# Tile 0's last product by column halves, with the second batch's attention spread through it

## The chip, the core and the metric

The kernel runs on one core of one Trainium2 chip. The core has a tensor engine (TensorE, PE in the profile: matmuls; its weight loads are shown as PEld), a vector engine (DVE), a scalar engine (ACT), a general engine (GpSimd, shown as POOL) and an engine that only issues transfers here (SyncE, SP). Sixteen DMA engines carry the transfers. Data lies in SBUF (128 partitions); matmuls write to PSUM, eight banks of 128 partitions by 512 fp32 values.

The metric is the device time of one execution, in microseconds. Before the change it is 351.59, the median of 3 runs (351.44 to 352.12).

## The reference

Attention over 8 batches and 8 heads, 576 tokens of width 64, causal by blocks of 64, then a gated feed-forward layer over all 4608 tokens.

```python
scores = scale * np.matmul(q, k.transpose(0, 1, 3, 2))   # q, k, v: (8, 8, 576, 64)
mask = block_i >= block_j                                # blocks of 64 positions
scores = np.where(mask, scores, -1000000000.0)
attn = np.exp(scores - np.max(scores, axis=-1, keepdims=True))
attn = attn / (np.sum(attn, axis=-1, keepdims=True) + 1e-09)
attn_out = np.matmul(attn, v)
x = attn_out.transpose(0, 2, 1, 3).reshape(4608, 512)
gate = np.maximum(x @ w_gate, 0.0)                       # w_gate, w_val: (512, 1536)
val = x @ w_val
return (gate * val @ w_out).astype(np.float32)           # w_out: (1536, 512)
```

All inputs and the output are float32; the kernel multiplies in bf16.

## The kernel before

**Tiles and steps.** The 512 first tokens of batch j make up tile j (0 to 7); the last 64 tokens of all batches make up a ninth tile. The feed-forward work is a generator, `ffn_gen` (L942), that hands out TensorE's matmuls one step at a time. Tile 0 has 144 steps: 96 products with the gate and value weights (L948: for each of 12 blocks of d_ff four gate products and four value products, the gate through ACT's relu at L958, their product on DVE at L968 as `hT`), and then 48 out products (`out_mm`, L1180) of 128 tokens by 512 columns: `hT` against `wo`, the bf16 copy of w_out. A finished group of 12 is copied by DVE to a buffer `ob` (`finish`, L1189) and stored later (`put`, L657; for tile 0 through the list `late`, from ACT's queue). In tile 0 the 48 run as groups two at a time, a third of the inner dimension in turn (L1201).

**The attention of later batches is spread between the steps.** The order is written out by hand for all five engines. A dictionary `AT` (L1338) gives each act a place, counted in steps; a loop at the end (L1780) emits the acts by place, and `ffn` (L1227) emits the steps that lie between. Places below 0 are before the first step. `HOW` (L1581) names the engine and the PSUM banks of each act. The names that matter here:

- `Lq`, `Lv`, `E1q`, `E1v`, `E2q`, ...: loads of q, k and v of batches 0, 1, 2 from SP's queue; `w{i}{g}` (i = 0 to 2, g = 0, 1): loads of w_out (`load_w_out`, L389); `T0` to `T2`: loads of the batches' tails. All loads go into a pool of ten staging buffers.
- `cq`, `cv`, `cg`, `cw`, `ev`, `q4`, `q6`, `tc`: casts of such loads to bf16, mostly on POOL (L198, L223, L231, L397).
- `m{hp}` (`mains_1`, L1329): TensorE transposes of q and k of a pair of heads of batch 1 (L284), with the copies out of PSUM (L293).
- `p{r}{i}` (`part`, L424): for batch 0, scores and exponential in three parts. `s{r}` and `e{r}`: for later batches the scores of a pair of heads (`visit`, L442; TensorE at L465) and their exponential on ACT (L470, L477). r is 4 x batch + pair of heads, so batch 1 has r = 4 to 7. Two parts of the scores go to the two double banks "sc"; the third goes, one half each, to two banks that `thirds` (L436) names.
- `c{r}`: memsets of the masked corners (`corners`, L523; L1241). `a{r}`, `b{r}`: the products with v of the first and second head (`head_av`, L626; L600) and the division by the row sum on DVE (`normalise`, L533; L537, L539). `x{r}`: the transposes into `xT`, the input of the feed-forward layer (`to_xT_pe`, L636, or by DMA).
- `l3`, `lv3`: batch 3's loads, issued by POOL (L353). `W`, `D`: sums of w_out's quarters on POOL (L706, L709) and differences on DVE (L720), for tiles 7 and 8, which use a product scheme with fewer multiplications.

**PSUM.** Two double banks ("sc"), one bank "one", three banks "ffn" that rotate. Gate and value products use ffn banks and, for some value products, "one" or "sc".

**Queues.** SP issues its loads in the written order; a load also waits for the eighth load before it. POOL works through its casts in order, so a late load holds all casts behind it.

The function that loads and casts w_out:

```python
    def load_w_out(i, g):
        return load_w(
            wo[i][:, 2 * g : 2 * g + 2],
            moe_w_out[512 * i + 256 * g : 512 * i + 256 * g + 256],
        )
```

Of the kernel before, what the change touches and what calls it, by code (L numbers as in the profile page):

```python
# [17 lines left out]
def kernel(  # L18
# [10 lines left out]
    nc = tc.nc  # L29
# [359 lines left out]
    def load_w_out(i, g):  # L389
        return load_w(  # L390
            wo[i][:, 2 * g : 2 * g + 2],
            moe_w_out[512 * i + 256 * g : 512 * i + 256 * g + 256],
        )
# [42 lines left out]
    def thirds():  # L436
        return (
            psum_one.tile([128, 512], FP, name="one"),
            psum_ffn.tile([128, 512], FP, name="ffnp"),
        )  # L440

    def visit(r):  # L442

        b, hp = divmod(r, 4)
        at = attnT[r % 4]
        first = psum_sc.tile([128, 2, 512], FP, name="sc")
        second = psum_sc.tile([128, 2, 512], FP, name="sc")
        third = thirds()
        tails = b >= FIRST
        pieces = [(2, False), *((c, True) for c in range(4) if tails)]  # L450
        for c, tail in pieces + [(c, False) for c in (0, 1, 3)]:
            for hh in range(2):
                where = {
                    0: first[:, hh, :],
                    1: second[:, hh, 0:384],
                    3: second[:, hh, 384:512],
                    2: third[hh][:, 0:256],
                }
                if tail:
                    o = third[hh][:, 256 + 64 * c : 320 + 64 * c]  # L460
# [4 lines left out]
                nc.tensor.matmul(  # L465
                    o, kTm[b % 2][head_of(hh), c, hp, :], qT, start=True, stop=True
                )
# [12 lines left out]

        return exp_third, exp(first, 0), exp(second, 512)
# [460 lines left out]
    def ffn_gen():  # L942
        for j in range(B + 1):
# [245 lines left out]
            def finish(op, s, n0, n1):  # L1189
                ob = sb.tile([128, 512], FP, name="ob", bufs=5)[:, 0 : n1 - n0]  # L1190
                nc.vector.tensor_copy(ob, op)
                if store:
                    store.pop()()
                (store if j else late).append(lambda j=j: put(j, s, ob, n0, n1))
# [6 lines left out]
            groups = outs(j)  # L1201
            while groups:
                some = 2 if j == 0 and len(groups) == 4 else 1
                ops = [
                    psum_ffn.tile([128, 512], FP, name="ffnp")[:, 0 : n1 - n0]
                    for _, n0, n1 in groups[:some]
                ]
                for f0 in (0, 4, 8) if some == 2 else (0,):
                    for op, (s, n0, n1) in zip(ops, groups):
                        for f in range(f0, f0 + 4 if some == 2 else 12):  # L1210
                            out_mm(op, s, f, n0, n1)
                            if f == 11:
                                finish(op, s, n0, n1)
                            yield
                groups = groups[some:]
# [30 lines left out]
    with tc.manual_schedule(engines={E.PE, E.DVE, E.Activation, E.Pool, E.SP}):  # L1246
# [82 lines left out]
        def mains_1(hp):  # L1329
            engs, banks = HOW[f"m{hp}"]  # L1330
            if banks == "one":
                both = bank("one", BF)
                two = [both[:, 512 * t : 512 * t + 512] for t in range(2)]
            else:
# [6 lines left out]
            "cq4": -40,  # L1341
            "cq6": -39.5,
            "M1q": -39,
            "M1k": -38.5,
            "p01": -38,
            "c0": -37.5,
            "j3": -37,
            "p11": -36.5,
            "M2q": -36,
            "p10": -35.5,  # L1350
            "M2k": -35,
            "p12": -34.5,
            "j2": -34,
            "M3q": -33.5,
            "M3k": -33,
            "cv0": -32.5,
            "cv2": -32,
            "c1": -31.5,
            "p20": -31,
            "a0": -30.5,  # L1360
# [9 lines left out]
            "cg00/01": -25.5,  # L1370
            "p30": -25,
            "cv4a": -24.5,
            "cv4b": -24,
            "cg00/23": -23.5,
            "x1": -23,
            "p32": -22.5,
            "c2": -22,
            "c3a": -21.5,
            "c3b": -21,
            "cv6a": -20.5,  # L1380
            "a2": 3,
            "b2": 3.01,
            "cv6b": 3.02,
            "C1": 3.03,
            "a3": 6,
            "b3": 6.01,
            "x2": 6.02,
# [22 lines left out]
            "ev0a": 32.33,  # L1410
            "ev0b": 32.34,
# [18 lines left out]
            "w01": 32.1,  # L1430
            "w00": 32.11,
            "w11": 32.11,
            "w20": 32.12,
            "w10": 32.12,
            "E1v0": 32.16,
            "w21": 32.16,
            "E1q6": 32.19,
            "E1q4": 32.19,
            "E1v4": 32.19,
# [4 lines left out]
            "cw00": 32.3,  # L1444
            "cw10": 32.3,
            "cw01": 32.3,
            "cw21/0": 32.33,
            "cw11": 32.33,
            "cw20": 32.33,
            "q6": 32.36,  # L1450
            "q4": 32.36,
            "E2q4": 33.82,
            "ev4": 34.05,
# [9 lines left out]
            "cw21/1": 110.84,  # L1463
            "e4": 114.3,
            "c4": 116.83,
            "s5": 119.48,
            "a4": 120.37,
            "b4": 120.57,
            "e5": 121.28,
            "m2": 122.6,  # L1470
            "c5": 124.67,
            "E2v4": 125.35,
            "T2": 126.26,
            "a5": 127.05,
            "s6": 128.09,
            "e6": 128.35,
            "b5": 129.8,
            "c6": 131.42,
            "m3": 132.5,
            "x4": 135.4,  # L1480
            "x5": 135.8,
            "s7": 139.49,
            "a6": 139.55,
            "b6": 140.59,
            "e7": 141.27,
            "c7": 141.68,
            "x6": 145.48,
            "a7": 147.62,
            "b7": 147.81,
            "x7": 153,  # L1490
# [112 lines left out]
            "cw21/1": "dve",  # L1603
# [17 lines left out]
            "cw21/0": "pool",  # L1621
# [25 lines left out]
                for n in (  # L1647
                    "g00/01 g00/23 v00/01 v00/23 g01/01 g01/23 v01 g10 v10 g11 v11 "
                    "g20 v20 g21 v21/0 v21/1 w00 w01 w10 w11 w20 w21/0 w21/1"
# [165 lines left out]
```

## Time and profile before

| what | value |
|---|---|
| median of 3 runs | 351.59 us (351.44 to 352.12) |
| the profiled execution, its own time | 352.3 us |
| its span on the core | 350.5 us |
| mean granted TensorE clock | 0.999 |
| PE busy | 339.8 us (97%), 3210 instructions |
| DVE, ACT, POOL busy | 225.5 (64%), 185.2 (53%), 153.8 us (44%) |
| DMA | 50.02 MB, mean 143 GB/s |
| tile 0's first gate or value product, and the end of its last out product | 15.77 and 57.26 us |

The profile comes from one execution. Times in it are counted from the first instruction, in microseconds. "Busy" for an engine is the time in which at least one of its instructions ran; matmuls overlap in the pipeline, so the printed mean of one is longer than the distance from one to the next. In a line of a timeline the first two numbers are start and duration, followed by engine, line of the kernel, operation, output and inputs, shape and count; what stands in square brackets is the idle time before and what ended it.

Gate products (L948) are the largest group by time of all engines, 93.0 us in 338 recorded instructions; out products of the tiles that use L1181 take 23.2 us in 91.

### The profile page before, as it was taken

The page shows a single profiled execution, that of the slowest core. Times are in us where ns is not written, and L with a number is a line of the kernel's source. Part 1 is how long each engine was busy: PE and PEld are TensorE (multiplying, and loading weights), DVE is VectorE, ACT ScalarE, POOL GpSimd, SP SyncE. Part 2 cuts the span into 40 slices and gives each one's busy share as a digit, 9 for nine tenths or more (in the row PEclk, how much of TensorE's full clock was granted, in tenths as well). Part 3 has the DMA queues.
Part 4 walks back from the last instruction along what each step waited for, and adds up shares of the span by engine and source line. Part 5 has one row for each costly group of instructions (what it writes and reads, how often), then busy time and mean ns, then how long its engine had stood idle before and what let it go on. Part 6 is the DMA issues. An engine that isn't in the chain of part 4 may idle for free.

```text
span 350.5 us, 8275 instructions
## 1 busy us (share of the span) xinstructions
PE 339.8 (97%) x3210; PEld 208.2 (59%) x3254; DVE 225.5 (64%) x564; ACT 185.2 (53%) x297; POOL 153.8 (44%) x194
## 2 busy tenths in 40 slices
PE   8999999999999999999999999999999999999994
PEld 3544455545445568545855576556755687687673
DVE  4853455667529784467547772668567867986892
ACT  5933766687235862666355545555366525423521
POOL 2767556576598902590149203950300022213213
PEclk9999999999999999999999999999999999999999
DMA  8999989999999994999459974999510031003005
GB/s 240 295 353 373 352 224 248 222 148 155 184 185 153 144 182 98 138 147 169 62 134 141 104 135 123 127 131 150 121 47 17 16 94 50 2 2 121 1 2 120
DMA packets 155399, 50.02 MB, mean 143 GB/s; under 512 B 134464, under 2 KB 151744, under 8 KB 155360
## 3 DMA queue, kind: packets, MB, share of 16 engines
q0 software_dynamic: 70528, 8.98, 49.1%
q1 hardware_dynamic: 77520, 32.52, 44.0%
q10 hardware_dynamic: 7312, 8.00, 7.8%
q8 instruction: 25, 0.41, 0.5%
q14 instruction: 14, 0.11, 0.1%
HBM read 37.75 MB, written 9.44 MB: 135 GB/s over the span
## 4 chain that ended last, share of the span: by engine, by line
PE 77%; DMA 14%; POOL 3%; issue 2%; DVE 2%; ACT 1%; SPq 1%; POOLq 0%; ACTq 0%
PE ffnp L948 39%; PE ffnp L830 12%; PE one L830 5%; PE sc L1014 3%; DMA stage<-in_moe_w_out_dram 3%; PE sc L465 3%; DMA xT<-xnat 2%; DMA stage<-in_moe_w_val_dram 2%; PE one L465 2%; DMA stage<-in_v_dram 2%; DMA stage<-in_moe_w_gate_dram 2%; PE ffnp L600 2%; PE one L600 2%; PE ffnp L1181 2%; PE one L1014 2%
## 5 line engine op out<-in xcount | busy, mean ns | idle before, releaser
L958 ACT ACTIVATE gate_sb<-ffnp 128x512 bf16<-128x512 f32 x95 | 57.1, 605 | 74.8 <-PE ffnp L948 66.5
L948 PE MATMUL ffnp<-xT,wg 128*128 128x512 bf16 x338 | 93.0, 379 | 1.7 <-issue 0.6
L948 PE MATMUL ffnp<-xT,wv 128*128 128x512 bf16 x309 | 87.7, 380 | 1.0 <-DVE hT L968 0.3
L968 DVE TENSOR_TENSOR hT<-gate_sb,ffnp 128x512 bf16<-128x512 bf16 x76 | 51.9, 683 | 46.0 <-PE ffnp L948 27.0
L948 PEld LDWEIGHTS <-wv 128*128 128x128 bf16 x384 | 35.4, 98 | 38.2 <-issue 4.6
L470 ACT ACTIVATE attnT<-sc 128x1024 bf16<-128x1024 f32 x56 | 57.0, 1042 | 0.0
L948 PEld LDWEIGHTS <-wg 128*128 128x128 bf16 x384 | 35.7, 98 | 35.0 <-issue 1.7
L882 POOL TENSOR_TENSOR ob<-ob 128x512 f32<-128x512 f32 x7 | 9.6, 1370 | 101.7 <-ACT ob L879 53.3
L830 PEld LDWEIGHTS <-stage 128*128 128x128 bf16 x420 | 40.3, 98 | 6.0
L789 DVE TENSOR_TENSOR stage<-hT 128x512 bf16<-128x512 bf16 (+2 forms) x82 | 37.8, 493 | 0.9
L600 PEld LDWEIGHTS <-attnT 128*128 128x128 bf16 x640 | 26.7, 98 | 11.9 <-DVE attnT L1241 0.9
L830 PE MATMUL ffnp<-stage 128*128 128x256 bf16 x252 | 31.4, 273 | 0.0
L353 POOL DMA_DIRECT2D v_bf<-in_v_dram x30 | 24.1, 869 | 6.1 <-DVE recip L537 2.6
L477 ACT ACTIVATE attnT<-one 128x512 bf16<-128x512 f32 (+1 forms) x28 | 15.0, 536 | 21.1 <-PE ffnp L465 21.1
L353 POOL DMA_DIRECT2D q_bf<-in_q_dram x20 | 17.9, 907 | 16.7 <-DVE hT L968 9.7
L1181 PE MATMUL ffnp<-wo,hT 128*128 128x512 bf16 x91 | 23.2, 379 | 0.3
L465 PEld LDWEIGHTS <-kTm 64*128 64x128 bf16 x384 | 11.0, 94 | 15.1 <-issue 7.9
L1045 POOL TENSOR_TENSOR ob<-ob 128x512 f32<-128x512 f32 x6 | 7.6, 1266 | 23.2 <-ACT ob L1044 23.2
L353 POOL DMA_DIRECT2D k_bf<-in_k_dram x20 | 17.8, 927 | 0.0
L830 PEld LDWEIGHTS <-hT 128*128 128x128 bf16 x168 | 16.4, 98 | 1.9
L465 PE MATMUL sc<-qTm,kTm 64*128 64x512 bf16 (+1 forms) x168 | 16.8, 305 | 0.0
L879 ACT COPY ob<-ffnp 128x512 f32<-128x512 f32 x7 | 4.1, 585 | 22.1 <-PE ffnp L830 22.1
(194 smaller groups left out, 556.0 us busy)
## 6 DMA issues: line engine op xcount, KB each, us to landing
out_dram<-ob ACTq DMA_DIRECT2D x28, 256.0 KB, 2.3
stage<-in_moe_w_val_dram SPq DMA_DIRECT2D x6, 512.0 KB, 8.7
stage<-in_moe_w_gate_dram SPq DMA_DIRECT2D x6, 512.0 KB, 8.2
stage<-in_moe_w_out_dram SPq DMA_DIRECT2D x6, 512.0 KB, 10.5
q_bf<-in_q_dram POOLq DMA_DIRECT2D x20, 128.0 KB, 4.2
k_bf<-in_k_dram POOLq DMA_DIRECT2D x20, 128.0 KB, 5.2
v_bf<-in_v_dram POOLq DMA_DIRECT2D x20, 128.0 KB, 7.0
stage<-in_v_dram SPq DMA_DIRECT2D x19, 128.0 KB, 5.5
```

Of the source, the lines that this page charges most:

```text
L353: ins = nc.gpsimd.dma_start(dst, part_of)
L465: nc.tensor.matmul(o, kTm[b % 2][head_of(hh), c, hp, :], qT, start=True, stop=True)
L470: return lambda: nc.scalar.activation(at[:, :, lo : lo + 512], sc, AF.Exp, scale=scale)
L477: nc.scalar.activation(at[:, hh, 1024 : 1024 + w], third[hh][:, 0:w], AF.Exp, scale=scale)
L600: nc.tensor.matmul(av[:, p, :], at[:, col : col + 128], v_bf[b % 2][:, c, h, :], start=(p == 0), stop=(c == p), skip_group_check=True,)
L789: nc.vector.tensor_tensor(out=out.rearrange("p (c n) -> p c n", c=m), in0=a, in1=b, op=op)
L830: nc.tensor.matmul(to, sums.of(c)[which][:, 128 * p : 128 * p + 128], right, start=first, stop=(c == 5), skip_group_check=True,)
L948: nc.tensor.matmul(to, (wg, wv)[t][f // 4][:, c, 128 * (f % 4) : 128 * (f % 4) + 128], x[:, c], start=(c == 0), stop=(c == 3),)
L958: nc.scalar.activation(gate_sb, gate, AF.Relu)
L968: nc.vector.tensor_tensor(out=h, in0=gate_sb, in1=val, op=AX.mult)
L1014: nc.tensor.matmul(to[:, 256 * k : 256 * k + 256], left[:, c, 128 * k : 128 * k + 128], right[:, c], start=new and (k, c) == (0, 0), stop= ...
L1181: nc.tensor.matmul(op, hT[f][:, 128 * s : 128 * (s + 1)], wo[f // 4][:, f % 4, n0:n1], start=(f == 0), stop=(f == 11),)
```

## The change

Four things, in the order of the diff.

1. `load_w_out` loads 512 rows by 256 columns (4 x 256 elements to a partition, runs of 1 KB) instead of 256 rows by 512 columns (runs of 2 KB). A load is 512 KB either way. SP's order becomes: the three left halves, v's first half of batch 1, q and k of batch 1's last two pairs of heads, the right half of the first part, v's second half, the right halves of the second and third part. Before, all six loads of w_out stood ahead of these loads of batch 1. The casts on POOL follow in the new order; the last of them is no longer split with DVE.
2. Tile 0's out products are four groups of 24 matmuls of 256 columns: a group is a column half and two blocks of 128 tokens, all into one bank: "one" for the first three groups, an ffn bank for the last. A step is two of them. One copy on DVE ends a group, and `put_block` stores it (512 rows of 1 KB runs become 256 rows by 256 columns).
3. Batch 1's acts from `e4` to `x7` are at other places. Both halves of the third part of the scores are in ffn banks for batch 1. `m2` and `m3` use one ffn bank, with both copies on DVE (before on ACT). `x4` is copied by DVE (before ACT); the banks of `r4`, `r6` and `r7` differ.
4. Batch 0: `cv0` before `cq4` and `cq6`, `a0` before `p20` and `M3k`, `p32` before `p30`, `b2` a step later, `x2` before `b3`; the corner memsets `c1`, `c2`, `c3b` on POOL instead of DVE, `c3a` later.

From tile 1 on, all places are the same.

```diff
     def load_w_out(i, g):
-        return load_w(
-            wo[i][:, 2 * g : 2 * g + 2],
-            moe_w_out[512 * i + 256 * g : 512 * i + 256 * g + 256],
-        )
+        n = slice(256 * g, 256 * g + 256)
+        return load_w(wo[i][:, :, n], moe_w_out[512 * i : 512 * i + 512, n])
...
-    def thirds():
-        return (
-            psum_one.tile([128, 512], FP, name="one"),
-            psum_ffn.tile([128, 512], FP, name="ffnp"),
-        )
+    def thirds(r):
+        return [bank("ffn" if i or r // 4 == 1 else "one") for i in range(2)]
...
-            groups = outs(j)
+            for half, s0 in [(h, s) for h in range(2) for s in (0, 2)] if j == 0 else []:
+                op = bank("ffn" if (half, s0) == (1, 2) else "one")
+                order = [
+                    (f, s)
+                    for i in range(3)
+                    for s in (s0, s0 + 1)
+                    for f in range(4 * i, 4 * i + 4)
+                ]
+                for n, (f, s) in enumerate(order):
+                    nc.tensor.matmul(
+                        op[:, 256 * (s - s0) : 256 * (s - s0) + 256],
+                        hT[f][:, 128 * s : 128 * (s + 1)],
+                        wo[f // 4][:, f % 4, 256 * half : 256 * half + 256],
+                        start=(n == 0),
+                        stop=(f == 11),
+                        skip_group_check=True,
+                    )
+                    if n == 23:
+                        ob = sb.tile([128, 512], FP, name="ob", bufs=5)
+                        nc.vector.tensor_copy(ob, op)
+                        late.append(
+                            lambda s0=s0, half=half, ob=ob: put_block(
+                                0, s0 // 2, 256 * half, ob, 0, 2
+                            )
+                        )
+                    if n % 2:
+                        yield
+            groups = outs(j) if j else []
             while groups:
-                some = 2 if j == 0 and len(groups) == 4 else 1
...
-            "cq4": -40,
-            "cq6": -39.5,
...
+            "cv0": -40,
+            "cq4": -39.5,
+            "cq6": -39,
...
+            "M3q": -33,
+            "a0": -32.5,
+            "p20": -32,
+            "M3k": -31.5,
...
+            "w01": 32.132,
+            "E1v4": 32.135,
+            "cw21": 32.362,
+            "cw01": 32.352,
+            "ev4": 32.355,
+            "c5": 114,
+            "m3": 115,
+            "s6": 115.01,
+            "e6": 115.02,
+            "a5": 120,
+            "b5": 120.01,
+            "x4": 120.02,
+            "s7": 125,
+            "e7": 125.01,
+            "c6": 125.02,
+            "a6": 128,
+            "b6": 128.01,
+            "x5": 132,
+            "c7": 134,
+            "a7": 136,
+            "b7": 136.01,
+            "x6": 139,
+            "x7": 143,
+            "c4": 107,
+            "w00": 32.1,
+            "w10": 32.101,
+            "w20": 32.102,
+            "E1v0": 32.11,
+            "E1q4": 32.12,
+            "E1q6": 32.13,
+            "w11": 32.141,
+            "w21": 32.142,
...
+            "e4": 95.1,
+            "s5": 108.01,
+            "e5": 108.02,
+            "a4": 108.03,
+            "m2": 108.04,
+            "b4": 108.05,
...
-            "s5": 119.48,
-            "a4": 120.37,
-            "b4": 120.57,
...
-            "m2": (("act", "act"), ("sc", "ffn")),
-            "m3": (("act", "act"), "one"),
+            "m2": (("dve", "dve"), "ffn"),
+            "m3": (("dve", "dve"), "ffn"),
-            "r4": ("dve", "one", "ffn", ("act", "sc")),
+            "r4": ("dve", "ffn", "ffn", ("dve", "ffn")),
             "r5": ("dve", "ffn", "ffn", ("act", "ffn")),
-            "r6": ("dve", "ffn", "ffn", ("act", "sc")),
-            "r7": ("dve", "sc", "one", ("dve", "one")),
+            "r6": ("dve", "ffn", "ffn", ("act", "one")),
+            "r7": ("dve", "one", "sc", ("dve", "one")),
...
-            "c1": "dve",
-            "c2": "dve",
+            "c1": "pool",
+            "c2": "pool",
             "c3a": "dve",
-            "c3b": "dve",
+            "c3b": "pool",
```

More of the change, by code (lines that the diff above doesn't have):

```diff
@@ L447, in visit @@
         second = psum_sc.tile([128, 2, 512], FP, name="sc")
-        third = thirds()
+        third = thirds(r)
         tails = b >= FIRST
@@ L1193, in finish @@
                     store.pop()()
-                (store if j else late).append(lambda j=j: put(j, s, ob, n0, n1))
+                store.append(lambda j=j: put(j, s, ob, n0, n1))
             if j >= SEVEN:
@@ L1199, in ffn_gen @@
                 continue
-            groups = outs(j)
-            while groups:
-                some = 2 if j == 0 and len(groups) == 4 else 1
[L1204 to L1215, printed above, removed]
+            for half, s0 in [(h, s) for h in range(2) for s in (0, 2)] if j == 0 else []:
[25 more added lines that the diff above has]
+                        yield
@@ L1217, in outs @@
+            groups = outs(j) if j else []
+            while groups:
+                s, n0, n1 = groups.pop(0)
+                op = psum_ffn.tile([128, 512], FP, name="ffnp")[:, 0 : n1 - n0]
+                for f in range(12):
+                    out_mm(op, s, f, n0, n1)
+                    if f == 11:
+                        finish(op, s, n0, n1)
+                    yield
     def outs(j):
@@ L1330, in mains_1 @@
             engs, banks = HOW[f"m{hp}"]
-            if banks == "one":
-                both = bank("one", BF)
+            if isinstance(banks, str):
+                both = bank(banks, BF)
                 two = [both[:, 512 * t : 512 * t + 512] for t in range(2)]
@@ L1340 @@
             "p02": -40.5,
-            "cq4": -40,
-            "cq6": -39.5,
[L1343 to L1360, printed above, removed]
+            "cv0": -40,
+            "cq4": -39.5,
+            "cq6": -39,
+            "M1q": -38.5,
+            "M1k": -38,
+            "p01": -37.5,
+            "c0": -37,
+            "j3": -36.5,
+            "p11": -36,
+            "M2q": -35.5,
+            "p10": -35,
+            "M2k": -34.5,
+            "p12": -34,
+            "j2": -33.5,
+            "M3q": -33,
+            "a0": -32.5,
+            "p20": -32,
+            "M3k": -31.5,
+            "cv2": -31,
+            "c1": -30.5,
             "p21": -30,
@@ L1369 @@
             "cv00/23": -26,
[L1370 to L1374, printed above, removed]
-            "x1": -23,
[L1376 to L1380, printed above, removed]
+            "c2": -25.5,
+            "cg00/01": -25,
+            "p32": -24.5,
+            "cv4a": -24,
+            "cv4b": -23.5,
+            "x1": -23,
+            "p30": -22.5,
+            "c3b": -22,
+            "cv6a": -21.5,
+            "cg00/23": -21,
+            "c3a": 3.5,
+            "w01": 32.132,
[30 more added lines that the diff above has]
+            "w21": 32.142,
+            "cw00": 32.3,
+            "cw10": 32.301,
+            "cw20": 32.302,
+            "ev0a": 32.33,
+            "ev0b": 32.331,
+            "q4": 32.34,
+            "q6": 32.35,
+            "cw11": 32.361,
+            "e4": 95.1,
[4 more added lines that the diff above has]
+            "b4": 108.05,
             "a2": 3,
-            "b2": 3.01,
+            "b2": 4,
+            "a3": 6,
+            "b3": 6.02,
+            "x2": 6.01,
             "cv6b": 3.02,
             "C1": 3.03,
-            "a3": 6,
-            "b3": 6.01,
-            "x2": 6.02,
             "x3": 8,
@@ L1409 @@
             "cv21/0": 32.24,
-            "ev0a": 32.33,
-            "ev0b": 32.34,
             "Lq0": -63.5,
@@ L1429 @@
             "E1q0": 20.29,
[L1430 to L1439, printed above, removed]
             "T0": 32.19,
@@ L1443 @@
             "q0": 32.24,
[L1444 to L1451, printed above, removed]
             "E2q4": 33.82,
-            "ev4": 34.05,
             "tc0": 34.05,
@@ L1462 @@
             "E2v0": 109.09,
-            "cw21/1": 110.84,
-            "e4": 114.3,
-            "c4": 116.83,
-            "s5": 119.48,
-            "a4": 120.37,
-            "b4": 120.57,
-            "e5": 121.28,
-            "m2": 122.6,
-            "c5": 124.67,
             "E2v4": 125.35,
             "T2": 126.26,
[L1474 to L1490, printed above, removed]
             "td0": 156.81,
@@ L1602 @@
             "cv21/1": "dve",
-            "cw21/1": "dve",
             "cv00/01": "pool",
@@ L1620 @@
             "r3": ("one", "sc", "dve", "sc"),
-            "cw21/0": "pool",
             "cg00/01": "pool",
@@ L1648 @@
                     "g00/01 g00/23 v00/01 v00/23 g01/01 g01/23 v01 g10 v10 g11 v11 "
-                    "g20 v20 g21 v21/0 v21/1 w00 w01 w10 w11 w20 w21/0 w21/1"
+                    "g20 v20 g21 v21/0 v21/1 w00 w01 w10 w11 w20 w21"
                 ).split()
```

## The prediction

> **What bounds the kernel now.** I read the page first, its slices and the chain that ended last, then the windows, then the timelines of TensorE, POOL, DVE and ACT around the lines that the diff touches. The windows show, per stretch, its length, the busy time and instructions of PE, weight loads, DVE, ACT and POOL, then the granted clock, the DMA share and GB/s.
>
> ```profile
> PE   8999999999999999999999999999999999999994
> PEclk9999999999999999999999999999999999999999
> 22.00:36.80 14.80, 14.75 (x70) 6.70 (x70) 6.92 (x11) 5.94 (x10) 9.31 (x10) 1.00 1.07 370
> 40.80:61.60 20.80, 20.42 (x198) 11.31 (x200) 10.83 (x34) 13.30 (x23) 13.09 (x19) 1.00 1.00 245
> 108.00:339.00 231.00, 229.15 (x2176) 147.77 (x2203) 159.36 (x396) 120.80 (x197) 81.49 (x90) 1.00 0.93 96
> ```
>
> TensorE is busy 339.8 of 350.5 us at the full clock. So only two things change the time: TensorE's own work, and its gaps. From 40.80 to 61.60, where the rewritten out products lie, only 0.38 of 20.80 us are gaps; the DMA share is 1.00, so no load there can arrive sooner without another arriving later. TensorE's timeline gives the prices and the gaps (start, duration, engine, line, operation, tiles, count; a matmul's printed duration is longer than its slot, so I use start to start).
>
> ```profile
> 36.86 0.39 PE L284 MATMUL one<-ident,k_bf 128*128 128x128 bf16 x4
> 37.08 0.81 PE L948 MATMUL ffnp<-xT,wv 128*128 128x512 bf16 x3
> ...
> 40.87 5.34 PE L1181 MATMUL ffnp<-wo,hT 128*128 128x512 bf16 x23
> 46.15 0.28 PE L465 MATMUL one<-qTm,kTm 64*128 64x256 bf16 x1
> 46.27 0.60 PE L465 MATMUL sc<-qTm,kTm 64*128 64x512 bf16 x6
> ...
> 54.67 0.60 PE L465 MATMUL sc<-qTm,kTm 64*128 64x512 bf16 x6
> 55.41 0.46 PE L600 MATMUL ffnp<-v_bf,attnT 128*128 128x65 bf16 x10
> ```
>
> A 512-column matmul takes 0.2157 from start to start (the four gate products from 38.39, the next at 39.25), so the first 23 out products should span 22 x 0.2157 + 0.38 = 5.13; the line shows 5.34: **gap one, 0.21**, at 42.82, where the products reach a quarter of w_out that POOL has only just cast (it casts four of them back to back from 41.17, for 3.75). **Gap two, 0.24**, lies before 55.41: a6 waits for v's cast (54.30 to 55.36), whose load was issued at 46.85 and landed at 53.80.
>
> **Part 1, start-up (batch 0's order).** It moves memsets from DVE to POOL and puts x2 ahead of b3. DVE's gaps on TensorE between 17.5 and 19.7 (0.37 + 0.12 + 0.21) mostly go; I estimate 0.3 us earlier. POOL had stood idle 0.83 before its cast at 21.33, which covers the memsets (0.17 to 0.31 on DVE) put ahead of it. But the k transposes at 36.86 start 0.09 after ACT's cast of that k (35.73 + 1.04), whose load landed at 35.71; the start-up edits do not touch that load. Whatever is won before is waited away there: 0. Bounds: -0.2 (some of the load's lead follows) to +0.3 (a worse order, nothing between absorbs a loss).
>
> **Part 2, the out products of tile 0.** 48 matmuls of 512 columns become 96 of 256. A slot of 256 columns is 2.62 / 24 = 0.1092 (the tile products at L830, 24 of them from 137.26), so 96 x 0.1092 - 48 x 0.2157 = **+0.13**. The four stores stay four of 256 KB, issued at the same later places of ACT's queue, which has gaps there: 0.
>
> **Part 3, the loads.** Runs of 1 KB instead of 2 KB. The casts that follow landings show both: with 1 KB (half-column gate and value weights) one per 1.50 us, with 2 KB one per 1.34.
>
> ```profile
> 24.35 1.04 POOL L397 CAST wv<-stage 128x1024 bf16<-128x1024 f32 x1 [0.47 <-DMA stage<-in_moe_w_val_dram]
> 25.85 1.04 POOL L397 CAST wg<-stage 128x1024 bf16<-128x1024 f32 x1 [0.46 <-DMA stage<-in_moe_w_gate_dram]
> 27.35 1.04 POOL L397 CAST wv<-stage 128x1024 bf16<-128x1024 f32 x1 [0.46 <-DMA stage<-in_moe_w_val_dram]
> 28.70 1.04 POOL L397 CAST wg<-stage 128x1024 bf16<-128x1024 f32 x1 [0.31 <-DMA stage<-in_moe_w_gate_dram]
> 30.03 1.04 POOL L397 CAST wv<-stage 128x1024 bf16<-128x1024 f32 x1 [0.30 <-DMA stage<-in_moe_w_val_dram]
> ```
>
> The first w_out load landed near 37.1. Estimated landings after, by these rates and by v's 0.4 to 0.5 for each 128 KB and q's and k's 0.72 for each 256 KB: left halves 37.2, 38.7, 40.2; v's first half 42.0; q and k of both pairs 44.9; w01 46.4; the rest of v 48.2; w11 49.7; w21 51.2. Each cast takes 1.04. The first group needs its third left half at 40.87 + 16 x 0.109 = 42.6 and has it at 41.3: gap one goes, **-0.21**. v's second half is ready by 49.3 and a6 wants it near 52.7: gap two goes, **-0.24**. The second half of w_out is the tight one: w11 is ready at 50.8 and wanted at 51.06, w21 at 52.3 and 53.28. I cost that at 0; it is hidden by the visits and AV heads moved in between.
>
> **Part 4, banks and hand-offs on the new order.** I laid TensorE's instructions out from 40.87 to tile 1's first product in bank "one" (61.63 before): 96 out products, three visits of 0.745, eight AV heads of 0.305, two transposes of a head pair at 0.45, four of xT at 0.22, 16 products at 0.2157: 20.39 against 20.26 before. These waits are new:
> - s4's second third now takes an ffn bank, and waits for ACT's gate there:
>
> ```profile
> 39.45 0.60 ACT L958 ACTIVATE gate_sb<-ffnp 128x512 bf16<-128x512 f32 x1 [0.49 <-PE ffnp L948]
> 45.61 0.69 DVE L1191 COPY ob<-ffnp 128x512 f32<-128x512 f32 x1 [1.15 <-PE ffnp L1181]
> 46.38 0.31 DVE L1241 MEMSET attnT<- 64x128 uint32 x2
> ```
>
>  It ends at 40.05, and 0.065 pass until TensorE goes on (the hand-off in this trace between an engine's end and its waiter): 40.11 against 40.00, **+0.11**.
> - Group (1,0) writes the bank "one" that group (0,2) held. From that group's last matmul: 0.31 to its end, 0.69 for DVE's copy (row above), 0.065: 1.065, against 0.93 of a5, b5 and x4 in between: **+0.13**.
> - a7 waits for c7's memset (0.31), queued on DVE behind group (1,0)'s copy: 1.40 against 1.20 of work in between, **+0.23** (0.20 to 0.26).
> - Tile 1's first value product takes the bank of group (1,2), whose copy stands on DVE behind x7's: 1.25 against 0.97, **+0.27**.
> - s6, 0.03, for the scores of s5 in the same banks.
> Added: 0.77. All are sums of durations in DVE's and ACT's rows against laid-out slots; the smallest they can be is 0 (each cover is within 0.3 of enough), the largest I give 1.3 (a hand-off that misses pushes DVE's next). Moving four copies of 0.58 to 0.65 from ACT to DVE at 0.69 is in these sums.
>
> A rule speaks against this part: the Trainium skill, Perfetto Trace Analysis, section Matmuls, has independent groups rotate through PSUM banks, so that one is evacuated while the next runs. Three of the four groups here use one bank; with nothing between them the two hand-offs would each cost 1.065 - 0.31 = 0.75, 1.4 more than in the sum. The order puts AV heads and a visit between, so I follow the rows.
>
> **Part 5, what comes earlier.** After tile 1's start the order is as before, but POOL and SP finish this group some 2.5 us sooner (51.2 against 53.80 for the last landing). Three later gaps hang on that: the visit of the tails at 63.36 (0.16, a product on DVE behind casts); the xT transpose by DMA, issued at 94.75 and landing at 103.45 (gap 103.28 to 103.50, 0.21); and this, where POOL is still at w_out's sums until 106.57 while DVE takes the differences, 1.53 for four against 0.88 for the next four, and TensorE waits 0.43 for hT behind them:
>
> ```profile
> 105.80 1.53 DVE L720 TENSOR_TENSOR wo<-wo 128x256 bf16<-128x256 bf16 x4
> 107.25 0.68 DVE L968 TENSOR_TENSOR hT<-gate_sb,ffnp 128x512 bf16<-128x512 bf16 x1
> 108.40 0.88 DVE L720 TENSOR_TENSOR wo<-wo 128x256 bf16<-128x256 bf16 x4
> 107.98 1.02 PE L948 MATMUL ffnp<-xT,wv 128*128 128x512 bf16 x4 [0.27 <-DVE hT L968]
> ```
>
> POOL's batch-3 loads start at 75.30 now, at 71 to 73 then; the sums end 2.5 to 3 earlier, before the differences begin. **-0.16, -0.21, -0.43.** Bounds: -1.1 (0.3 more of start-up lead reaches here) to 0 (the lead is eaten on the way).
>
> **Sum.** +0.13 - 0.45 + 0.77 - 0.80 = -0.35. The profiled execution takes 352.3 (span 350.5 and 1.8 around it), 0.7 above the median of the three runs, 351.59; the change is the same on both: 351.95 for a profile, **351.2** for the median.
>
> **Rivals.**
> *Slower: the late half of w_out.* Place: group (1,0), ninth matmul. One of the 16 DMA queues falls behind: of the loads at issue 46.85 fifteen parts were in at 51.16 and the last at 53.80, 2.6 later; of the load before it, 48.36 and 49.36, 1.0. If w11's last part lands after 49.95 (51.06 - 1.04 - 0.065) everything behind it on POOL is late too, and TensorE has nothing else in order. With 49.7 + 1.0 the price is 0.75, with 49.7 + 2.6 it is 2.35; I take 1.6: 351.24 + 1.6 = 352.8. For it: cover of 0.25 only, and runs half as long. Against: the lag in the trace strikes the 256-byte runs of v, and w11 comes behind them only by one load.
> *Hand-offs cost nothing.* Part 4 is worked to 0.1 us with slots that drift; each lacks 0.3 or less of cover, and any one wait upstream supplies it to those behind. 0.64 of the 0.77 goes: 350.6.
> *The lead does not arrive.* The change shortens tile 0 but the batch-3 loads on POOL wait for other things (buffers that come free with tile 1's visits); then part 5 keeps only 0.16: 351.24 + 0.64 = 351.9. The change does then nothing measurable.
>
> **How the numbers follow.** Chances: forecast 0.34, hand-offs free 0.26, lead lost 0.12, late w_out 0.28. 0.2%, about what a measurement here can tell from no change, is 0.70 us: faster means below 350.89, slower above 352.29. The forecast's own spread, 350.7 to 351.8, gives a third of it to faster; the second case does mostly, the third is same, the fourth slower in nine of ten. Faster 0.11 + 0.23 = 0.34, slower 0.25 + 0.03 = 0.28, same 0.38. The range runs from 350.3 (hand-offs free, part 5 at its best) to 353.2 (a late w11 at 2 us); beyond lie the 2.6 us lag and a start-up loss on top.
>
> **What would show it.** No gap within the first out group; a6 without a wait on POOL; waits of 0.1 to 0.3 before s4's second third, group (1,0), a7 and tile 1's first value product, each released by ACT or DVE; tile 1's first product in "one" 0.4 to 0.5 later than 61.63 counted from 40.87; POOL's first batch-3 issue near 72 and the first four differences near 0.9. The forecast is wrong if TensorE stands at the ninth matmul of group (1,0) with POOL as releaser, or if the k transposes do not start near 36.86.

## The result, and the profile after

| | before | after |
|---|---|---|
| median of 9 runs | 351.44 us (351.23 to 352.12) | 354.01 us (352.98 to 356.9) |
| ratio to before | | 1.0084, 95% interval 1.0065 to 1.0103 |
| the profiled execution, its own time | 352.3 us | 353.58 us |
| its span | 350.5 us | 351.8 us |

The change makes the kernel slower, by 2.6 us between the medians. It also makes its time spread over 3.9 us, where the kernel before spreads over 0.9.

The windows of the kernel after, in the same columns as those of before (length, busy time and instructions of PE, weight loads, DVE, ACT, POOL; clock, DMA share, GB/s), lie around the start of the loads, tile 0's out products, and the rest:

```profile
22.00:36.80 14.80, 14.71 (x68) 6.56 (x68) 6.60 (x11) 5.96 (x11) 9.25 (x10) 1.00 1.08 362
41.20:63.60 22.40, 20.93 (x248) 15.83 (x248) 13.55 (x38) 10.94 (x18) 12.62 (x18) 1.00 1.11 255
108.00:340.00 232.00, 230.10 (x2195) 148.28 (x2220) 160.28 (x400) 121.01 (x196) 81.60 (x90) 1.00 0.96 95
```

Only the second has lost: 1.47 of its 22.40 us are gaps. TensorE's timeline has the gap in one place (a bracket gives the idle time and what ended it):

```profile
50.16 0.39 PE L636 MATMUL ffnp<-ident,xnat 128*128 128x128 bf16 x4
50.50 1.05 PE L1205 MATMUL one<-wo,hT 128*128 128x256 bf16 x8
52.94 0.38 PE L1205 MATMUL one<-wo,hT 128*128 128x256 bf16 x2 [1.39 <-POOL wo L395]
53.25 0.28 PE L460 MATMUL ffnp<-qTm,kTm 64*128 64x256 bf16 x2
```

After eight products of group (1,0) TensorE stands: from the eighth to the ninth start 1.66 us pass instead of 0.11, so 1.55 are lost. POOL's timeline and the chain of waits say for what:

```profile
47.98 1.04 POOL L395 CAST wo<-stage 128x1024 bf16<-128x1024 f32 x1 [0.97 <-DMA stage<-in_moe_w_out_dram]
50.52 1.06 POOL L223 CAST v_bf<-stage 128x1024 bf16<-128x1024 f32 x1 [1.50 <-DMA stage<-in_v_dram]
51.84 1.04 POOL L395 CAST wo<-stage 128x1024 bf16<-128x1024 f32 x1 [0.26 <-DMA stage<-in_moe_w_out_dram]
54.03 1.04 POOL L395 CAST wo<-stage 128x1024 bf16<-128x1024 f32 x1 [1.15 <-DMA stage<-in_moe_w_out_dram]
```
```profile
46.42 0.16 DVE kTm L293
46.58 5.21 DMA stage<-in_moe_w_out_dram
51.79 0.05 issue
51.84 1.05 POOL wo L395
52.90 0.04 issue
52.94 0.38 PE one L1205 x2
```

The third cast is that of w11. POOL is idle before it and starts it 0.05 after the load is in, at 51.79: not POOL is late but the load. It was issued at 46.58 only. SP's timeline, after and, in the second fence, before:

```profile
26.47 6.17 SPq L371 DMA_DIRECT2D stage<-in_moe_w_out_dram  x3
...
42.15 4.33 SPq L162 DMA_DIRECT2D stage<-in_v_dram  x4
46.58 2.13 SPq L371 DMA_DIRECT2D stage<-in_moe_w_out_dram  x2
```
```profile
26.55 7.30 SPq L371 DMA_DIRECT2D stage<-in_moe_w_out_dram  x6
34.28 7.33 SPq L162 DMA_DIRECT2D stage<-in_v_dram  x4
```

SP, which takes 0.41 to 0.5 for a load when nothing holds it, needs 6.17 for three loads of 1 KB runs and 4.33 for the four of v ahead of w11; before, it issued six of 2 KB runs in 7.30. Between these issues lie some 0.1 us or less, so the time goes into the issuing itself. I take it that SP's queue is full of pieces that the 16 DMA engines have not taken yet; no run tests that. Nor does the late issue alone explain the landing: w11 was in 1.42 after the load before it, no more than the 1.50 at which loads of 1 KB runs follow each other.

### The profile page after: what moved, and what is told of

It reads as the page before. It is cut to its first block, busy times and chain, and to the rows that moved or that the text cites. A ratio compares the mean times of both kernels' runs of the same rounds, so it can differ in the third digit from the quotient of the medians.

```text
span 351.8 us, 8382 instructions
## 1 busy us (share of the span) xinstructions
PE 340.8 (97%) x3261; PEld 213.3 (61%) x3302; DVE 226.8 (64%) x563; ACT 182.9 (52%) x292; POOL 156.7 (45%) x199
## 4 chain that ended last, share of the span: by engine, by line
PE 91%; ACT 2%; DVE 2%; DMA 1%; issue 1%; POOL 1%; POOLq 0%
PE ffnp L943 45%; PE ffnp L825 12%; PE one L825 5%; PE sc L1009 3%; PE sc L460 3%; PE ffnp L1176 3%; PE one L460 2%; ACT attnT L427 2%; PE one L595 2%; PE ffnp L595 2%; PE one L1009 2%; PE one L943 2%; DMA stage<-in_moe_w_out_dram 1%; PE one L1248 1%; PE one L1205 1%
## 5 line engine op out<-in xcount | busy, mean ns | idle before, releaser
L877 POOL TENSOR_TENSOR ob<-ob 128x512 f32<-128x512 f32 x7 | 9.6, 1370 | 99.6 <-ACT ob L874 51.2
L353 POOL DMA_DIRECT2D q_bf<-in_q_dram x20 | 18.1, 913 | 21.9 <-DVE hT L963 9.7
L472 ACT ACTIVATE attnT<-one 128x512 bf16<-128x512 f32 (+1 forms) x24 | 13.5, 561 | 16.6 <-PE ffnp L460 16.5
L472 ACT ACTIVATE attnT<-ffnp 128x512 bf16<-128x512 f32 (+1 forms) x32 | 16.0, 514 | 5.8 <-PE ffnp L460 5.8
L460 PE MATMUL sc<-qTm,kTm 64*128 64x512 bf16 (+1 forms) x168 | 16.8, 305 | 0.0
```

What stands on the lines that cost most here:

```text
L353: ins = nc.gpsimd.dma_start(dst, part_of)
L460: nc.tensor.matmul(o, kTm[b % 2][head_of(hh), c, hp, :], qT, start=True, stop=True)
L472: nc.scalar.activation(at[:, hh, 1024 : 1024 + w], third[hh][:, 0:w], AF.Exp, scale=scale)
```

## The experiments

All ratios are to the kernel before on the same chip.

| kernel | median us | ratio, 95% interval |
|---|---|---|
| before_again, after_again (one run each) | 352.51, 353.21 | |
| new_start | 351.56 | 1.0003, 0.9994 to 1.0012 |
| d_later | 351.54 | 1.0000, 0.9991 to 1.0009 |
| old_start | 353.85 | 1.0085, 1.006 to 1.011 |
| w11_first | 353.97 | 1.0069, 1.005 to 1.0087 |
| v_last | 352.69 | 1.0036, 1.0022 to 1.005 |
| v_last_old | 352.76 | 1.0041, 1.0029 to 1.0052 |
| v_later | 352.76 | 1.0035, 1.0022 to 1.0048 |
| v_later_banks | 353.43 | 1.0057, 1.0036 to 1.0079 |
| before_1kb | 352.41 | 1.0028, 1.0016 to 1.004 |
| after_2kb | 353.62 | 1.0075, 1.0044 to 1.0106 |
| v_last_2kb | 352.22 | 1.0025, 1.0014 to 1.0035 |

### Is the first profile of before typical?

**before_again**, no edit.

> The kernel before once more, for a second profile. Theory A: the two late gaps of the first profile (0.21 at 103.3 for the xT transpose, 0.43 at 107.6 behind the four slow differences) belong to that one execution, which took 352.3 where the median is 351.4. Then they are not here, w_out's sums on POOL end near 102 and not at 106.6, and the profiled time is about 351.6. Rival B: they come each time, the sums end near 106.6, and the profiled time is 352.2 or so.

It took 352.51. TensorE's timeline and DVE's:

```profile
41.24 5.13 PE L1181 MATMUL ffnp<-wo,hT 128*128 128x512 bf16 x23
63.97 0.41 PE L503 MATMUL sc<-qTt,kTm 64*128 64x64 bf16 x16 [0.47 <-DVE hT L968]
```
```profile
106.04 1.51 DVE L720 TENSOR_TENSOR wo<-wo 128x256 bf16<-128x256 bf16 x4
108.61 0.88 DVE L720 TENSOR_TENSOR wo<-wo 128x256 bf16<-128x256 bf16 x4
```

The slow differences are here again, as rival B had it. The other gaps are not where they were: the out products take 5.13 without a stop, a6 follows its predecessor without a gap, the xT transpose is in time, and instead 0.64 are lost at 63.3. But this execution, too, is 1.0 above the median, so the question stayed open.

**d_later** makes the clash impossible.

```diff
-            AT[f"D{c}"] = 306 + 4 * c
+            AT[f"D{c}"] = 326 + 4 * c
```

> The kernel before with nothing changed but w_out's differences on DVE, 20 steps later (326 + 4 c in place of 306 + 4 c), so that POOL's sums are done in any case. Theory A (the clash of 0.43 in the first profile belongs to executions near 352.4, not to the median): the median stays at 351.4 to 351.6. Rival B (every execution has it): it falls by 0.4 to 351.1, and this version beats both kernels.

351.54, ratio 1.0000: theory A. Executions at the median do not have the 0.43. **new_start** shows such a one: the profiled execution took 351.51, and in its timeline the first four differences are as fast as the next.

```profile
105.47 0.89 DVE L720 TENSOR_TENSOR wo<-wo 128x256 bf16<-128x256 bf16 x4
...
107.43 0.88 DVE L720 TENSOR_TENSOR wo<-wo 128x256 bf16<-128x256 bf16 x4
```

### Does the start-up count?

**new_start** is the kernel before with batch 0's places and the engines of `c1`, `c2`, `c3b` of the kernel after; **old_start** is the opposite, the kernel after with those of before. The core of it, as new_start has it:

```diff
-            "b2": 3.01,
-            "b3": 6.01,
-            "x2": 6.02,
+            "b2": 4,
+            "b3": 6.02,
+            "x2": 6.01,
```

> The kernel before with batch 0's order and engines of the changed one, and nothing else. Theory A (x2 ahead of b3 keeps b3 and so x3 waiting, 0.34, and nothing behind it takes it up): the k transposes start near 37.2 and the median is 351.8. Rival B (the waits of 0.2 for w_out and 0.24 for v, which come from loads, shrink by what TensorE is late): 351.4 to 351.5.

> The changed kernel with batch 0's order and engines as before. Theory A (the loads set the end of tile 0): batch 1's k transposes are back at 36.86, 0.34 earlier, but the right half of w_out lands when it did, so the wait in group (1,0) grows by the same 0.3 to about 1.9, and the median stays at 354.0. Rival B (start-up loss and wait add up): the median falls by 0.34 to 353.7. Rival C (start-up is the main part of the loss, other than the profile shows): it falls by over 1 us.

new_start: k transposes from 37.2 on, median 351.56, no difference from before (351.50 on the same chip; rival B has 351.4 to 351.5, theory A 351.8). Its window over tile 0's out products is full:

```profile
41.20:61.60 20.40, 20.40 (x201) 11.05 (x200) 10.79 (x34) 13.21 (x23) 13.10 (x19) 1.00 1.04 258
```

TensorE begins the out products 0.3 later than in the first profile of before and ends them at the same time, since the two waits for loads (0.21 and 0.24 there) are gone. But the old order, too, can begin them that late: at 41.24 in before_again, at 41.17 in d_later. old_start: the out products start at 40.91 instead of 41.30, the ninth product of group (1,0) at 53.00 instead of 52.94, after a wait of 1.73 instead of 1.55; the interval of its ratio lies over that of the kernel after (theory A). The start of tile 0 does not set its end here; the load does.

What the start-up edit itself does, the timeline of the kernel after seems to show:

```profile
18.55 0.40 PE L636 MATMUL sc<-ident,xnat 128*128 128x128 bf16 x4 [0.20 <-DVE xnat L534]
18.79 0.47 PE L595 MATMUL sc<-v_bf,attnT 128*128 128x65 bf16 x10
19.10 0.39 PE L943 MATMUL one<-xT,wv 128*128 128x512 bf16 x1
19.99 0.40 PE L636 MATMUL sc<-ident,xnat 128*128 128x128 bf16 x4 [0.50 <-DVE xnat L534]
```

x2 waits, and b3, put behind it, starts at 18.79 (18.20 before), so its division on DVE comes later and x3 at 19.99 instead of 19.65. In new_start, though, b3 waits for something else than x2. TensorE's timeline and ACT's:

```profile
18.77 0.47 PE L600 MATMUL sc<-v_bf,attnT 128*128 128x65 bf16 x10 [0.23 <-ACT v_bf L231]
```
```profile
18.30 0.42 ACT L231 CAST v_bf<-stage 128x256 bf16<-128x256 f32 x1 [1.88 <-DMA stage<-in_v_dram]
```

It waits for the cast of v's last part, and ACT for that load. The load is in at 18.28 in new_start and at 18.19 in the kernel after, where the cast ends at 18.64; in the kernel before it was in at 16.91. Fifteen of its 16 parts are in by 17.1 in all three; one DMA engine is late. So it is in all nine profiles with the new start-up order (18.1 to 18.3) and in none of the six with the old one (16.8 to 17.0); why, no run shows. Nor is x3's delay certain: x3 starts from 19.82 to 20.03 in the new order, from 19.52 to 20.03 in the old.

### One late load, or all of them?

**after_again**, no edit.

> The changed kernel once more, for a second profile. If the loss is the wait for the right half of w_out's second part, TensorE stands again at the ninth matmul of group (1,0), between 0.8 and 3 us, for POOL's cast, and the profiled time moves with the landing of that load one to one: time = 352.0 + the wait. If the wait of 1.55 was a chance of the first profile, it is under 0.5 here and the time is lost elsewhere.

353.21, with the wait at the same product: 1.23. That is 352.0 + 1.2, as expected: in these two profiles the time follows this one wait. Both lie below the median of 354.01, so what the slower executions wait for is not in them.

**w11_first**:

```diff
-            "w11": 32.141,
-            "cw11": 32.361,
+            "w11": 32.1325,
+            "cw11": 32.3525,
```

> The changed kernel with the right half of w_out's second part loaded, and cast, ahead of the second half of v. It lands about 2.4 us earlier (four v loads of 0.6), at 49.4, and the wait at the ninth matmul of group (1,0) is gone. Theory A (all these loads together are late, the last one lands at 54 whatever their order, and 8.5 us of TensorE work stand behind the last w_out part): the wait moves to the 17th matmul of that group or to a6, 1 to 1.5 us long, and the median is 353.6 to 354.1. Rival B (only this one load was late): no wait over 0.4 takes its place and the median is 352.4.

The median, 353.97, is theory A's: nothing is won. The profile has no wait at the ninth product, and two others:

```profile
52.36 0.83 PE L1205 MATMUL one<-wo,hT 128*128 128x256 bf16 x6
54.23 0.76 PE L595 MATMUL ffnp<-v_bf,attnT 128*128 128x65 bf16 x20 [1.04 <-POOL v_bf L223]
56.02 1.03 PE L1205 MATMUL one<-wo,hT 128*128 128x256 bf16 x8 [1.03 <-POOL wo L395]
```

w11 is in at 48.58 and group (1,0) runs through its ninth product, but a6 waits for v and the 17th for w21. How long these waits are at the median is not shown: this execution took 355.69, 1.7 above it, and one DMA engine was far behind the others (of w21, 15 parts were in at 52.50, the last at 54.87).

**v_last** keeps the amount of loads and gives TensorE other work while they come: v's second half is loaded last, and what needs it is put back.

```diff
-            "E1v4": 32.135,
+            "E1v4": 32.143,
...
-            "a6": 128,
-            "b6": 128.01,
+            "a6": 136,
+            "b6": 138,
...
-            "a7": 136,
-            "b7": 136.01,
+            "a7": 140.5,
+            "b7": 141,
```

> The changed kernel with the three right halves of w_out loaded and cast ahead of v's second half, and the four AV heads that need that v moved back by 8 to 10 steps (a6, b6, a7, b7 and x6, x7 near the places they had before the change). Theory A (the loads take the time they take; what counts is how much TensorE work has to stand behind the last one, 6.2 us before the change, 8.5 to 9 after it): the right halves land near 47.5, 49 and 50.5, group (1,0) does not wait, v lands near 53 and a6 waits less than 0.5; tile 1's first product in bank one comes near 62.1 instead of 63.7, and the median is 352.4. Rival B (the half loads themselves are late, by their 1 KB runs): the wait in group (1,0) stays over 0.8 and the median is 353.4 or more.

352.69, 0.3 above theory A: half of the loss is gone. The loads did not come sooner (the last part of v was in at 53.76, that of w21 in the kernel after at 53.98); POOL's casts in v_last:

```profile
47.54 1.04 POOL L395 CAST wo<-stage 128x1024 bf16<-128x1024 f32 x1 [1.05 <-DMA stage<-in_moe_w_out_dram]
49.12 1.04 POOL L395 CAST wo<-stage 128x1024 bf16<-128x1024 f32 x1 [0.53 <-DMA stage<-in_moe_w_out_dram]
50.84 1.04 POOL L395 CAST wo<-stage 128x1024 bf16<-128x1024 f32 x1 [0.68 <-DMA stage<-in_moe_w_out_dram]
53.91 1.06 POOL L223 CAST v_bf<-stage 128x1024 bf16<-128x1024 f32 x1 [2.03 <-DMA stage<-in_v_dram]
```

Group (1,0) does not wait; a6 starts 0.20 late; tile 1's first product in "one" comes at 61.91 (63.70 in the kernel after). This execution took 352.07, 0.6 less than the median, so at the median more is lost than it shows.

**v_last_old**, v_last with batch 0's old order:

> The same, and batch 0's order as before the change. With the waits for loads gone, the start-up should show: 0.34 less than v_last, near 352.0 to 352.1, if it adds; the same as v_last if a load still sets the end of tile 0.

352.76, the same as v_last. In the profiled execution one DMA engine brought v's last part 0.9 after the 15th, at 54.67, and a6 waited 1.26.

**v_later**, with a6 to b7 and c7 at their places of before:

> v_last with a6, b6, a7, b7 and c7 at the very places they had before the change (139.55 to 147.81), so that some 6 us of TensorE work stand behind v, as before. Theory A (two causes: 1 KB runs, which cost the kernel before 0.9 by themselves, and the work behind the last load): the waits for v of 0.2 and 1.26 in the two earlier profiles go to under 0.3, and the median comes to 352.3 or 352.4, where the kernel before stands with 1 KB runs; what is left over the kernel before is the price of the runs and 0.2 to 0.3 of hand-offs. Rival B (something else in the new order costs the rest, the hand-offs of banks): it stays at 352.7, with no wait for a load.

352.76. No load is waited for any more, but two other waits stand in TensorE's timeline:

```profile
58.74 0.46 PE L595 MATMUL one<-v_bf,attnT 128*128 128x65 bf16 x10 [0.24 <-ACT xT L637]
64.67 0.41 PE L498 MATMUL sc<-qTt,kTm 64*128 64x64 bf16 x16 [0.36 <-DVE hT L963]
```

From start to start they cost 0.40 and 0.53: a bank hand-off that these places make, and a later consumer of late loads (next section). Theory A's waits for loads are gone, but the time is rival B's; of B's cause, hand-offs of banks, only the first wait is one. The two waits and the narrower matmuls (0.13) would make 1.06 of the 1.3 that are left over the kernel before.

**v_later_banks**, the same with the banks of r6's transposes and of a7 and b7 as before:

> v_later with the banks of the kernel before for the last two pairs of heads (the xT transposes of r6 in sc, a7 in sc and b7 in one), since its profile shows a wait of 0.40 before a7 for ACT's copy out of bank one. Theory A (that wait came from the places that I chose, and is not hidden): the wait is gone and the median is 352.3 to 352.4. Rival B (DVE's late tail casts, 0.53 at 64.1, take up what is won): 352.7.

353.43, with times from 352.38 to 356.33: nothing won. The profiled execution, at 354.35, waited 0.96 for w21 and 1.46 at 64.7. Whether the hand-off alone is worth 0.4 can't be told from this.

### The width of the runs

**before_1kb**: the kernel before, each w_out load in runs of 1 KB.

```diff
-        return load_w(
-            wo[i][:, 2 * g : 2 * g + 2],
-            moe_w_out[512 * i + 256 * g : 512 * i + 256 * g + 256],
-        )
+        st = new_stage(1024).rearrange("p (h c n) -> p h c n", h=2, c=2)
+        rows = moe_w_out[512 * i + 256 * g : 512 * i + 256 * g + 256]
+        nc.sync.dma_start(st, rows.rearrange("(c p) (h n) -> p h c n", p=128, h=2))
+        dst = wo[i][:, 2 * g : 2 * g + 2].rearrange("p c (h n) -> p c h n", h=2)
+        return dst, st.rearrange("p h c n -> p c h n")
```

> The kernel before with its six w_out loads as they were, but each written in runs of 1 KB instead of 2 KB. Theory A (runs cost: 1.50 against 1.36 per load): the sixth load lands 0.8 later, the wait in the first out groups grows from 0.2 to some 0.9, the wait before a6 to about 0.5, and the median is 351.9 to 352.4. Rival B (bytes alone count): landings and median as before, 351.5.

352.41, 0.9 slower: theory A. SP's and TensorE's timelines:

```profile
26.51 10.94 SPq L392 DMA_DIRECT2D stage<-in_moe_w_out_dram  x6
```
```profile
43.79 1.89 PE L1182 MATMUL ffnp<-wo,hT 128*128 128x512 bf16 x8 [0.39 <-POOL wo L398]
45.87 1.24 PE L1182 MATMUL ffnp<-wo,hT 128*128 128x512 bf16 x5 [0.19 <-POOL wo L398]
```

SP needs 10.94 for the six instead of 7.30; the sixth is in at 44.90 instead of 43.95; the first 23 out products wait 1.18 in three places (0.27, 0.55, 0.35) instead of 0.21. The Trainium skill, Perfetto Trace Analysis, section DMA Optimizations, says that small transfers, under 2 KB, have a significant overhead each. A load here is 512 KB and only its runs are that short; read for runs, the trace agrees: from landing to landing of the first four loads 1.50 us pass against 1.35.

**after_2kb** and **v_last_2kb** take 2 KB runs in the changed order:

```diff
-        return load_w(wo[i][:, :, n], moe_w_out[512 * i : 512 * i + 512, n])
+        st = new_stage(1024)
+        rows = moe_w_out[512 * i + 256 * g : 512 * i + 256 * g + 256]
+        nc.sync.dma_start(
+            st.rearrange("p (c f) -> p c f", c=2),
+            rows.rearrange("(c p) f -> p c f", p=128),
+        )
+        return wo[i][:, :, n], st.rearrange("p (c f) -> p c f", c=4)
```

> The changed kernel, all orders as they are, but each w_out load fetches 256 whole rows in 2 KB runs instead of 512 half rows in 1 KB runs, and is put where the half columns go: w_out's values stand in wrong places, so the output is another one; bytes, loads, casts and matmuls are the same. Theory A (runs and order are two separate prices): SP issues sooner and each load takes 1.36 instead of 1.50, the right half of the second part lands 0.7 to 1.0 earlier, the wait at the ninth matmul of group (1,0) is 0.3 to 0.9, and the median is 353.1, by the 0.9 that the same runs cost the kernel before. Rival B (the order alone sets it): 353.7 to 354.0. Rival C (the runs are all of it): under 352.2.

> v_last with the same 2 KB loads (w_out's values stand in wrong places here too). Theory A: both prices are gone, what is left over the kernel before is the narrower matmuls and hand-offs, 0.2 to 0.4: the median is 351.7 to 351.9, and a6 does not wait. Rival B (hand-offs and moved visits cost more than that): 352.3 or more.

353.62 and 352.22, 0.4 and 0.5 under their pairs with 1 KB, each between its theories and nearer to rival B. Their intervals overlap those of their pairs, so neither gain is shown; in the profile of after_2kb w11 was in 1.0 sooner and its wait 0.60, but the wait for w21 was 1.12 then. The profiled execution of v_last_2kb, 353.08, waits for no load and still loses 1.45 in one place:

```profile
65.01 0.41 PE L504 MATMUL sc<-qTt,kTm 64*128 64x64 bf16 x16 [1.29 <-DVE hT L969]
```
```profile
61.24 1.04 DVE L217 CAST v_bf<-stage 64x256 bf16<-64x256 f32 x1
62.82 0.50 DVE L210 CAST k_bt<-stage 64x256 bf16<-64x256 f32 x1 [0.53 <-POOL q_bt L209]
63.35 0.29 DVE L217 CAST v_bf<-stage 64x256 bf16<-64x256 f32 x1
63.67 0.69 DVE L969 TENSOR_TENSOR hT<-gate_sb,ffnp 128x512 bf16<-128x512 bf16 x1
```

These are the casts of the tails, loads that stand behind batch 1's on SP. They hold DVE's queue, the `hT` products behind them are late, and TensorE waits for the banks. In new_start POOL is done with its part of them at 60.0, and DVE's four take 0.29 each.

## Why the prediction was wrong

Two steps failed, and they add up to nearly all of the error.

**Part 3, w11 "at 0, hidden by the visits and AV heads".** The last row of the estimated landings was wrong: w11 was in at 51.79, not 49.7, w21 at 53.98, not 51.2. Up to v's first half the estimates hold to 0.3 (37.15, 38.67, 40.44 and 42.20 measured). Then q and k took until 46.34 (44.9), and v's second half, at 0.6 for each 128 KB instead of 0.4 to 0.5, until 50.37 (48.2). Of the 2.1 that w11 was late, q and k brought 1.4 and v 0.6; w11 itself followed at the estimated rate. The estimate let each load follow the last at the rate of the bytes, from a DMA share of 1.00. That share is a mean: before, from 44.0 to 44.5 it is 0.44 and from 53.0 to 53.5 it is 0.12.

The rival of the late half of w_out named the place, the ninth product of group (1,0), and the price, 1.6 against 1.55 and 1.23 measured. That the price fits is in part luck: its cause, one DMA engine behind the others, made 0.5 of it, as 15 parts of w11 were in at 51.30 and the last at 51.79; all of them were late. Its argument against, that the lag strikes v's runs of 256 bytes, was a misreading: 48.36 and 49.36 belong to the load of q issued at 44.27. It had a chance of 0.28, and its time, 352.8, was still 1.2 too low, for the second reason.

**The sum, "the change is the same on both".** The profiled execution lay 0.7 above the median. I took gains from the gaps in it (-0.45 in part 3, -0.80 in part 5) and set the sum against the median, which does not have these gaps: new_start, profiled at the median, has neither the waits in the out products nor the clash with POOL's sums, and d_later wins nothing by making the clash impossible. Without these 1.25 the rival's sum is 351.44 + 0.13 + 0.77 + 1.6 = 353.9. The measured median is 354.01. That they meet so closely is luck too: with the measured 1.55 and 0.40 (part 4 below) the sum is 353.4, near the profiled execution's 353.58, and the 0.4 by which the median lies above that is in no profile.

By the other steps:
- *Part 1, start-up 0.* The total was right: new_start and old_start show no difference. But there were no 0.3 to be won and waited away: b3 waits for a load that comes 1.3 later, and x3 starts no sooner than in the old order.
- *Part 2, narrower matmuls.* Group (0,0) ran its 24 in the 2.62 that was taken.
- *Part 4, hand-offs 0.77.* Group (1,0) started 0.12 late (0.13 predicted), tile 1's first value product 0.19 (0.27), s4's second third 0.1 (0.11); a7 and s6 did not wait; I take it that the wait in group (1,0) gave DVE time. Some 0.4 of 0.77, so the rival by which 0.64 of it costs nothing is half right. Between new_start and the kernel after, from 41.2 to tile 1's first product in "one", TensorE needs 22.40 instead of 20.45: 1.55 for w11 and 0.40 for all the rest.
- *Part 5.* POOL's batch-3 issues did not start at 71 to 73 but at 76.89, and the last landing came at 53.98, not 2.5 sooner than 53.80. The first four differences were at 0.89 all the same, as in new_start.
- *The lead does not arrive* (0.12) was not put to the test: tile 0 became longer, so there was no lead.

What the change costs then: v_last shows that 1.3 of the 2.6 are the order, TensorE's work that needs no load being spent too early. Behind the last w_out part stand 8.5 us of work (55.17 to 63.70); before, behind the last v, 6.2 (55.41 to 61.63). In the first profile of before the loads end when they do in the kernel after (53.80 and 53.98), but that is the profile that is not typical. POOL's cast of the last v in new_start, at the median:

```profile
52.77 1.06 POOL L223 CAST v_bf<-stage 128x1024 bf16<-128x1024 f32 x1 [2.31 <-DMA stage<-in_v_dram]
```

In new_start and d_later this load is in at 52.63 and 52.73, so the change also makes the last load about 1 us later; with 1 KB runs alone (before_1kb) it is in at 53.43. The run width costs 0.9 in the kernel before. In the changed order its price is not shown (0.4 and 0.5, within the noise). If it is 0.9 there too, 0.4 is left for the narrower matmuls, hand-offs and later waits; these runs do not separate them, and the cause of this second half of the loss stays in part open.

No version here beats the kernel before; new_start and d_later equal it.

## What to carry to other kernels

Where many loads follow each other closely, their order can't be judged load by load: find the time of the last one, from more than one profile, and count the work that has to stand behind it. Taking away one wait may only show the next consumer of the same stream (w11, then v and w21, then the tail casts).

Compare a profile's own time with the median before reading gains from its gaps: a gap that belongs to an execution 0.7 us slow is nothing that a change can win.

Before a wait is put down to an edit, look at what ended it, and at how much the same place moves between executions without the edit: b3 stands behind x2 in the new order, but in new_start it waits for a load.

## What the runs showed of the hardware

SP's issue of one load took from 0.41 to 2.5 us. With the same bytes, six loads took SP 7.30 in 2 KB runs and 10.94 in 1 KB runs, while the first four landings went from 1.35 to 1.50 apart. That SP is held up by what the DMA engines have still before them fits these times, but is not tested.

One DMA engine can lag behind the 15 others by 0.9 to 2.7 us for a few loads: the last part of a load of v was in at 53.80, the 15th at 51.16. It strikes other loads in other executions: w21 in w11_first (355.69, 1.7 above its median), w21 and v in v_later_banks (354.35, 0.9 above). That it makes the wide spread of the kernel after, which has little cover behind its loads (352.98 to 356.9, against 351.23 to 352.12), is likely from this but not shown.

DVE can be slowed by POOL's work in SBUF. The cast of v's tail (L217, 64x256) took 0.29 in new_start at 61.72, with POOL idle, and 1.04 in v_last_2kb during a cast on POOL at 61.10 to 62.14. It does not strike each overlap: at 63.35 there DVE's took 0.29 again, and POOL's cast beside it 0.56 (0.41 in new_start). The four differences took 0.88, and 1.51 to 1.53 while POOL's sums ran. The Trainium skill, Perfetto Trace Analysis, section Optimizing Scalar/DVE Operations, has the two engines share a read port, with which these rows agree.
